# One order table replaced by another: the items of phase one of a pooled attention and Strassen FFN kernel, with more matmuls ahead of the fourth inner step

## The chip, the cores and the metric

The kernel runs on one core of one Trainium2 chip. Its engines are TensorE (PE in the profile, its weight loads PEld), VectorE (DVE), ScalarE (ACT), GpSimd (POOL) and SyncE (SP, which here only issues DMAs). The metric is the device time in microseconds of one execution. The kernel before takes 905.62 us, the median of three runs (904.5 to 905.83).

## The reference

Attention with pooled keys and values, eight batches of eight heads, 576 positions of 64; then a feed-forward layer whose activation is h + sin²(alpha h)/alpha. Cut to what matters, all in float32:

```
q, k, v: (8, 8, 576, 64)
k_p = k.reshape(B, H, 72, 8, D).mean(axis=3)        # 576 keys become 72
v_p = v.reshape(B, H, 72, 8, D).mean(axis=3)
attn = softmax(q @ k_p.T / sqrt(D))                 # 576 x 72 for each head
x = (attn @ v_p) rearranged to (4608, 512)          # 8 batches of 576 tokens, 8 heads of 64
h = x @ w_in                                        # w_in 512 x 2048
g = h + sin(alpha * h)**2 / (alpha + 1e-9)
out = g @ w_out                                     # w_out 2048 x 512
```

## The kernel before, in words

**Two phases.** Phase one computes the attention and, with its output x, the first product h and the activation g, which is stored to memory. Phase two (`outputs`, products at L1294) loads g again and multiplies it by w_out. In the profiled execution phase two begins at 513 us on TensorE. Only phase one is ordered by the table that is changed, apart from a few preparations for phase two (`"R"`: loads and sums that are begun in the last units of phase one).

**Strassen.** The first product is done on blocks of 512 tokens (nine *units* u) and slices of w_in (four values J for each unit). One (u, J) is a *group*, n = 4u + J, 36 in all. A group is a 2 by 2 block product by Winograd's form of Strassen: seven products `M1` to `M7` in place of eight. In each, four parts `M{p}.{i}` (L975) are one matmul instruction each, float32, 128x128 weights and 256 columns; the trace has two records for each. The sums of weights that the products need are made once, the sums of x by `sums_of_x` (L939, VectorE, items `sx` and `sn`). The products share PSUM banks: product 6 is added to a copy of product 1 (`c16`, L950, ScalarE), product 7 to a copy of that (`c67`), and `p5` copies product 5 out. Then come sums on VectorE (`a11`, `a01`, `a00`, `f10`, `f1`; L949), sines (`s..`, L1044) and squares (`q..`, L1051) on ScalarE, and the store of g (`st`, SP).

**The inner level.** In units 1 to 6 products 1 and 5 of some groups are themselves done by seven smaller products (`inner_products`, L1053 on): J=0, 2 and 3 do both, J=1 does product 1 alone. The steps are

- `i.a`: two inner products for each of them into a spare bank (TensorE, L1066)
- `i.ca` and `i.cm`: copies of these on ScalarE, into the result's bank (L1079) and to a buffer (L1083)
- `i.b`: two more, added to what `ca` copied (TensorE, L1066)
- `i.cb`: a copy of one quarter of the result to another (ScalarE, L1086)
- `i.d`: the third inner step on TensorE, added to what `cb` copied (L1066)
- `i.ad`: a sum on VectorE of what is there and what `cm` put aside (L1089)
- `i.e1`, `i.e5`: the fourth inner step on TensorE, added to what `ad` wrote (L1066), one item for product 1 and one for product 5

So each step on TensorE waits for a copy or a sum of what the step before wrote. Other groups' products stand between the steps on TensorE, and under them the copies run.

**The attention** of batch u+1 runs beside the groups of unit u: loads of k, v and q, pooling (`pool_k`, `pool_v`; L271, POOL), scores (L444), softmax (`shift`, `exp`, `norm`), turning of the weights (`turn`, then `move`: 16 DMAs at L650), values (L739, L752), output to x (`out`), and the next but one batch's q turned by VectorE and DMAs (`qa` to `qe`, L357 to L370). The first batch is done by its own finer items (`first_batch`, L1102): q, k and v in pairs of heads, on TensorE `q_head` (L532), `k_head` (L515), `k_last` (L521), `score` (L553), and `fill` (L1131), matmuls on ones whose results nobody reads, between them.

**What sets the order.** Nothing is left to a scheduler. Each item is put on one agenda with a key; `perform` sorts the agenda by the keys and issues the items in that order, and an engine does its instructions in the order of issue. The keys stand in the tables `ORDER` (L42 on). `"F"` is the first batch, `"U0"` the attention items of unit 0, `"U"` those of units 1 to 6, `"U7"` and `"R"` the end. A group's keys are counted from 7n and come from a table by its kind: `first0` to `first3` (unit 0), `enter` (n=4), `mid0` to `mid3` (groups 5 to 26 by their J: 5, 6, 6 and 5 of them), `exit` (n=27), `end0` to `end3` (units 7 and 8).

```
def perform(self, until):
    self.agenda.sort(key=lambda x: x[:2])
    while self.agenda and self.agenda[0][0] < until:
        self.agenda.pop(0)[2]()
```

Of the kernel before, what the change touches and what calls it, by code (L numbers as in the profile page):

```python
# [43 lines left out]
    "load_k0": -3.59252, "load_v": -0.96965, "scores0": 3.279, "shift1": 6.66681, "shift0": 7.14828, "scores1": 7.66855, "shift2": 7.69635,  # L44
    "exp1": 11.39419, "exp0": 11.40344, "shift3": 11.6083, "exp2": 11.66391, "exp3": 11.68798, "norm0": 11.85811, "norm1": 11.86021, "norm2": 11.9294,
    "norm3": 11.93036, "pool_k0": 11.93266, "pool_v": 11.93269, "pool_vm": 11.9327, "turn2": 12.15533, "turn1": 12.33183, "turn3": 12.34767,
    "load_q": 13.4176, "load_k1": 13.54022, "turn0": 15.964, "move": 24.04575, "clean": 24.12855, "qa": 24.12869, "values": 24.12873,
    "out4": 24.12875, "qb": 24.12884, "pool_k1": 24.12885, "out0": 24.12885, "mark": 24.12895, "qc": 24.129, "out2": 24.129, "sx0": 24.1291,
    "inner_x": 24.12915, "out3": 24.33175, "k_t": 24.4364, "k_c": 24.4956, "qd": 24.83712, "out1": 24.87145, "sx1": 24.87995, "qe": 24.96216,
    "sx2": 25.5786, "sx3": 33.62096},  # L50
"F": {
    "load_al": -7.89, "load_q0": -7.88, "sqrt": -7.52, "fill0": -7.4, "turn_al": -7.28, "root": -7.15637, "q_head0": -7.13171, "exp_t": -7.10741,
    "load_k0": -6.95386, "fill1": -6.86584, "load_kr": -6.77452, "refine": -6.57394, "load_k1": -6.56, "load_q2": -6.534, "load_k2": -6.33476,
    "load_k3": -6.22799, "add_k0": -6.06864, "add_r": -5.99534, "load_q4": -5.97084, "load_q6": -5.84, "load_v": -5.76726, "win0": -5.72,
    "k_head0": -5.42865, "k_last": -5.12, "add_k2": -4.77276, "add_k1": -4.54784, "zero_z4": -4.54071, "score0": -4.52, "add_k3": -4.46549,
    "q_head1": -4.4, "zero_tr": -4.37098, "shift0": -4.16, "k_head1": -4.11213, "exp0": -4.04, "fill2": -4.00595, "score1": -3.79101,
    "fill3": -3.70961, "q_head2": -3.56, "qrest": -3.47419, "shift1": -3.44, "exp1": -3.32, "norm0": -3.2, "norm1": -3.08, "fill4": -2.96,
    "k_head2": -2.83714, "k_head3": -2.67519, "q_head3": -2.67509, "vrows": -2.66442, "vrest": -2.65517, "score2": -2.32076, "shift2": -2.24,
    "ahead0": -2.12, "comb0": -2.0, "score3": -1.88, "exp2": -1.85875, "k1_0": -1.79183, "ahead1": -1.76, "shift3": -1.52, "norm2": -1.4,
    "exp3": -1.28, "norm3": -1.16, "values": -1.11464, "load_q1": 0.04, "k1_1": 0.05858, "pool_k0": 1.1349, "win1": 1.89886, "comb1": 1.92786,  # L60
    "comb2": 1.98213, "pool_k1": 3.78556},
"U0": {
    "vsum": 1.50081, "qrest": 1.50141, "ahead": 1.502, "load_v": 2.08618, "pq0": 2.15962, "win3": 2.42169, "vals": 2.503, "sx2": 2.50351,
    "sx3": 2.50375, "score4": 2.504, "pq3": 2.82144, "win2": 2.94801, "pq4": 4.05233, "pq2": 4.0566, "pq1": 4.07221, "qt0": 4.511, "qt1": 4.51172,
    "kt0": 4.51227, "kc0": 4.96887, "scores0": 5.518, "shift0": 5.52, "shift1": 5.521, "comb1": 7.38091, "qt3": 7.92628, "qt2": 8.13953,
    "pool_vm": 8.75569, "qt4": 9.526, "exp1": 9.52613, "exp0": 9.52662, "scores1": 10.519, "shift2": 10.522, "norm0": 12.96627, "shift3": 13.00319,
    "comb2": 13.15659, "norm1": 13.38469, "turn0": 13.38824, "exp2": 14.22682, "exp3": 15.56789, "exp4": 15.57472, "load_k0": 16.01154,
    "load_q": 16.43872, "norm2": 16.65626, "load_k1": 16.66341, "norm3": 16.67159, "comb3a": 16.67343, "turn1": 16.69456, "comb3b": 16.77826,
    "turn3": 17.03674, "turn2": 17.289, "nrest": 17.37323, "move1": 18.86855, "move2": 18.96992, "clean": 18.98312, "move0": 19.548, "arest": 21.5955,
    "qc": 21.89678, "pool_v": 22.64595, "w2_1": 22.78383, "pool_k1": 22.83011, "pool_k0": 22.88021, "qa": 23.561, "qb": 23.562, "qd": 23.84216,  # L70
    "vrest": 26.13943, "values": 26.551, "qe": 26.565, "out0": 26.7312, "out2": 26.9598, "mark": 26.9713, "w2_5": 27.34755, "sn0": 27.5,
    "inner_x": 27.55453, "out1": 27.76959, "out4": 27.8955, "out3": 27.97572, "kt1": 28.19418, "sn2": 28.3493, "sn1": 28.40019, "kc1": 28.50762,
    "sn3": 28.51},
"U7": {
    "sn0": 27.5, "sn2": 27.50625, "sn1": 27.51, "sn3": 28.24964},
"R": {
    "w0": 8.86895, "w1": 11.17262, "w2": 11.21326, "w3": 7.30011, "w4": 17.42295, "w5": 22.96478, "w6": 15.7898, "w7": 16.74706, "w8": 20.6,
    "w9": 22.47405, "w10": 23.6, "v0": 6.6, "v1": 12.9421, "v2": 13.6, "v3": 16.48877, "v4": 17.6, "v5": 20.79675, "g0": 5.5, "i0": 20.16574,
    "i1": 27.65493, "i2": 27.65286, "i3": 27.6628, "o0": 20.58574, "o1": 25.65, "o2": 27.65},
"end0": {  # L80
    "M1.2": -2.57294, "M1.0": -2.53472, "M1.1": -2.45741, "M1.3": -2.25355, "c16": -1.1367, "M5.0": -0.09345, "M5.1": 0.9728, "M2.0": 1.17425,
    "M6.0": 1.17485, "M2.1": 1.21724, "M6.2": 1.21765, "M5.2": 1.21779, "M6.1": 1.21784, "M6.3": 1.21789, "M5.3": 1.21819, "M2.2": 1.21845,
    "c67": 2.29615, "M2.3": 2.3555, "M7.0": 2.35565, "p5": 2.384, "s00": 2.38414, "q00": 2.3842, "M7.1": 2.5708, "M7.2": 2.57295, "M3.2": 3.16644,
    "M3.0": 3.47531, "M3.1": 3.63665, "M7.3": 3.7191, "M3.3": 4.06192, "a00": 6.599, "a11": 6.59915, "M4.0": 6.82409, "a01": 6.89334, "M4.1": 7.01225,
    "M4.2": 7.0125, "s11": 7.04685, "s01": 7.11736, "M4.3": 7.14095, "s10": 7.149, "q1": 7.19287, "q01": 7.22535, "f10": 8.3468, "f1": 8.63666,
    "st": 10.05},
"end1": {
    "M5.0": -3.33019, "M5.1": -2.72125, "M1.0": -0.17668, "M5.2": -0.17606, "M1.1": -0.17602, "M1.2": -0.06105, "M1.3": -0.0, "M5.3": 0.01245,
    "c16": 0.08171, "M6.1": 0.14395, "M6.0": 0.15524, "M6.2": 0.1611, "p5": 0.19815, "M6.3": 0.2009, "M2.1": 0.2077, "c67": 0.20789, "M2.2": 0.20881,
    "M2.3": 0.20922, "M2.0": 0.20955, "s00": 0.3, "q00": 0.3002, "a00": 2.19325, "M7.1": 2.79825, "M3.0": 2.80473, "M7.0": 2.81351, "M7.3": 2.88245,  # L90
    "M7.2": 2.88791, "M3.1": 2.88955, "M3.2": 2.9988, "M3.3": 3.21335, "a11": 3.46515, "s11": 4.32131, "M4.0": 4.4354, "a01": 5.1294, "M4.1": 7.91733,
    "M4.2": 7.92785, "M4.3": 7.99325, "s10": 8.1665, "q1": 8.17037, "s01": 8.2013, "q01": 8.36455, "f10": 9.25247, "f1": 9.6345, "st": 10.05},
"end2": {
    "M5.0": -5.21769, "M5.1": -4.19849, "M1.0": -3.17899, "M1.1": -2.75025, "M1.2": -2.51525, "M1.3": 0.90215, "M5.2": 0.99395, "M5.3": 0.99415,
    "c16": 1.14695, "p5": 1.1828, "M6.0": 1.4299, "M2.0": 1.4318, "M6.2": 1.43214, "M2.1": 1.43255, "M2.2": 1.5857, "M6.1": 1.71475, "M6.3": 1.7193,
    "M2.3": 1.7196, "c67": 1.78765, "s00": 1.78813, "q00": 1.79224, "M7.1": 2.3807, "M3.0": 2.38083, "M7.0": 2.38084, "M7.2": 2.38085, "M7.3": 2.3819,
    "a00": 2.69669, "a11": 2.7835, "M3.1": 3.71335, "M3.2": 3.93591, "M3.3": 5.35825, "M4.0": 5.57345, "a01": 5.76695, "M4.3": 6.28487,
    "M4.1": 6.46705, "M4.2": 7.97136, "s11": 9.31248, "s10": 9.36555, "q1": 9.36695, "s01": 9.43775, "q01": 9.4416, "f1": 9.6118, "f10": 9.90706,
    "st": 10.05},
"end3": {  # L100
    "M5.0": -5.29345, "M5.1": -4.88305, "M1.2": -2.23625, "M1.0": -1.54834, "M1.3": -1.48014, "M5.2": -1.2153, "M1.1": -1.21312, "c16": 2.27975,
    "M6.2": 2.3529, "M6.0": 2.35688, "M6.1": 2.35962, "M2.1": 2.36295, "M2.0": 2.3654, "M6.3": 2.3726, "c67": 2.37425, "M2.2": 2.4012,
# [1468 lines left out]
```

## Time and profile before

| | |
|---|---|
| time, median of three runs | 905.62 us (904.5 to 905.83) |
| span of the profiled execution | 902.2 us |
| time less span (median) | 3.4 us |
| PE busy | 894.0 us, 99% |
| DVE, ACT, POOL busy | 678.2, 457.3, 206.5 us |
| phase two on TensorE | from 513.33 us, 384.23 us |

The page gives the span of one execution and no time of its own for it, so the median stands for it. A row of a timeline has the start, the length, the engine, the line, the operation with its tiles (output <- inputs), its shape and how many instructions it holds, and in brackets how long the engine was idle before and what released it. Matmuls overlap in such rows: a matmul's length is longer than the distance to the next one's start, so the distance between starts is what a matmul costs. In rows of waits the columns are the line that waited, what it waited for, the total in us, the number of times and the longest.

### The profile page before, as it was taken

To read this page: it belongs to the slowest core of one execution; us is meant where nothing else is said; L and a number is where in the kernel's file an instruction comes from. 1 tells how busy PE (TensorE), PEld (TensorE's weight loads), DVE (VectorE), ACT (ScalarE), POOL (GpSimd) and SP (SyncE) were. 2 spreads that over 40 slices of the span, in tenths; PEclk is the share of its full clock that TensorE was granted. 3 is DMA by queue.
4 is the path that set the end of the run, shared out by engine and by line. 5 is a ranking of instruction groups with operands and counts; after the bars stand their busy time and mean duration, and the time that the engine had idled before them with its cause. 6 is when DMAs were issued, how large, how long until landed. Compare 5 with 4: busy or idle time off the path is not lost.

```text
span 902.2 us, 18350 instructions
## 1 busy us (share of the span) xinstructions
PE 894.0 (99%) x7146; PEld 815.0 (90%) x7146; DVE 678.2 (75%) x1016; ACT 457.3 (51%) x1073; POOL 206.5 (23%) x235
## 2 busy tenths in 40 slices
PE   8999999999999999999999999999999999999997
PEld 5787888978888898888888899999999999999997
DVE  7576857668586684854466999979798888889894
ACT  5696878868787787786885611211111111111111
POOL 4969561814418164130000000000000000000000
PEclk9999999999999999999999999999999999999999
DMA  9956766666766666645426346261618172534401
GB/s 271 229 170 181 209 193 177 209 173 200 212 179 197 198 187 173 175 133 200 181 104 213 99 152 193 65 191 35 224 30 231 31 201 63 171 92 130 134 15 40
DMA packets 128751, 141.17 MB, mean 156 GB/s; under 512 B 46920, under 2 KB 95704, under 8 KB 128664
## 3 DMA queue, kind: packets, MB, share of 16 engines
q1 hardware_dynamic: 125880, 137.88, 52.6%
q10 hardware_dynamic: 2784, 2.11, 0.9%
q8 instruction: 57, 0.93, 0.4%
q14 instruction: 30, 0.25, 0.1%
HBM read 75.37 MB, written 47.19 MB: 136 GB/s over the span
## 4 chain that ended last, share of the span: by engine, by line
PE 98%; DVE 1%; DMA 0%; ACT 0%; issue 0%; ACTq 0%
PE PS L1294 43%; PE PS L975 41%; PE PS L1066 7%; PE PS L444 2%; PE PS L739 2%; PE PS L752 1%; DVE home L939 1%; DMA q<-in_q_dram 0%; PE PS L553 0%; PE PS L532 0%; PE PS L1131 0%; PE PS L416 0%; PE PS L697 0%; PE PS L343 0%; PE PS L695 0%; PE PS L607 0%
## 5 line engine op out<-in xcount | busy, mean ns | idle before, releaser
L975 PE MATMUL PS<-home,a 128*128 128x256 f32 x968 | 250.3, 382 | 0.0
L975 PEld LDWEIGHTS PS<-home,a 128*128 128x128 f32 x968 | 177.3, 190 | 28.6 <-issue 4.7
L975 PE MATMUL PS<-home,as 128*128 128x256 f32 x728 | 194.9, 381 | 0.9 <-DVE home L939 0.9
L975 PEld LDWEIGHTS PS<-home,as 128*128 128x128 f32 x728 | 134.1, 190 | 18.3 <-DVE home L939 0.9
L1294 PE MATMUL PS<-s,wb 128*128 128x144 f32 x896 | 119.1, 286 | 0.0
L1294 PEld LDWEIGHTS PS<-s,wb 128*128 128x128 f32 x896 | 113.6, 190 | 0.0
L1051 ACT ACTIVATE s<-s,c 128x256 f32<-128x256 f32 (+1 forms) x216 | 112.7, 580 | 0.0
L1344 POOL TENSOR_TENSOR cc<-cc,cb 128x576 f32<-128x576 f32 x1 | 2.0, 1974 | 483.1 <-DVE cb L1249 483.1
L949 DVE TENSOR_TENSOR h<-PS,s 128x512 f32<-128x512 f32 x72 | 49.5, 687 | 70.3 <-ACT s L1051 70.3
L1430 ACT COPY PS<-PS 128x144 f32<-128x144 f32 x56 | 14.7, 263 | 143.4 <-PE PS L1294 140.8
L1294 PE MATMUL PS<-r,wb 128*128 128x144 f32 x512 | 73.2, 286 | 0.0
L1294 PE MATMUL PS<-s,a 128*128 128x144 f32 x512 | 73.2, 286 | 0.0
L1044 ACT ACTIVATE s<-h,al 128x256 f32<-128x256 f32 x144 | 64.1, 502 | 16.4 <-DVE h L949 13.3
L271 POOL TENSOR_TENSOR kvin<-kvin 96x768 f32<-96x768 f32 (+3 forms) x42 | 69.9, 1665 | 3.1 <-DMA a<-in_moe_w_in_dram 0.6
L1294 PEld LDWEIGHTS PS<-r,wb 128*128 128x128 f32 x512 | 67.1, 190 | 0.1
L1294 PEld LDWEIGHTS PS<-s,a 128*128 128x128 f32 x512 | 67.1, 190 | 0.0
L949 DVE TENSOR_TENSOR h<-PS,p 128x512 f32<-128x512 f32 x72 | 49.1, 685 | 22.3 <-PE PS L975 21.7
L950 ACT COPY PS<-PS 128x512 f32<-128x512 f32 x72 | 41.4, 576 | 46.2 <-PE PS L975 23.0
L1044 ACT ACTIVATE s<-PS,al 128x256 f32<-128x256 f32 x144 | 60.3, 473 | 6.1 <-PE PS L975 5.8
L498 POOL TENSOR_TENSOR ex<-ex,sm 128x576 f32<-128x576 f32 (+1 forms) x28 | 35.2, 1270 | 109.8 <-DVE sm L497 108.9
L1412 ACT COPY PS<-PS 128x144 f32<-128x144 f32 x56 | 14.7, 263 | 88.7 <-PE PS L1294 88.7
L949 DVE TENSOR_TENSOR h<-h,s 128x1024 f32<-128x1024 f32 x36 | 44.8, 1246 | 14.2 <-ACT s L1051 14.1
(217 smaller groups left out, 1531.4 us busy)
## 6 DMA issues: line engine op xcount, KB each, us to landing
g_bridge<-h SPq DMA_DIRECT2D x72, 512.0 KB
r<-g_bridge SPq DMA_DIRECT2D x31, 1152.0 KB
out_dram<-o SPq DMA_DIRECT2D x122, 72.0 KB
kvin<-in_k_dram SPq DMA_DIRECT2D x14, 576.0 KB
q<-in_q_dram SPq DMA_DIRECT2D x7, 1024.0 KB
kvin<-in_v_dram SPq DMA_DIRECT2D x14, 512.0 KB
ex<-tr SPq DMA_DIRECT2D x54, 92.0 KB
ex<-tr SPq DMA_DIRECT2D x54, 88.0 KB
```

What stands on the lines that cost most here:

```text
L271: self.nc.gpsimd.tensor_tensor(out=t[..., 0:w] if w > D else out, in0=t[..., 0:w], in1=t[..., w:2 * w], op=OP.add)
L444: nc.tensor.matmul(ps[e][r0 + r:r0 + r + q.shape[-1], h, :], q[s], kb[s, hp, :], start=True, stop=True)
L498: nc.gpsimd.tensor_tensor(out=E(i), in0=E(i), in1=sm.unsqueeze(2).to_broadcast([P, n, Sp]), op=OP.mult)
L739: nc.tensor.matmul(o[r:r + 64], w, x, start=start and i < 2, stop=False, skip_group_check=True)
L949: add = lambda o, x, y: nc.vector.tensor_tensor(out=o, in0=x, in1=y, op=OP.add)
L950: copy = lambda o, x: nc.scalar.copy(out=o, in_=x)
L975: nc.tensor.matmul(ps[:, jj, :], self.A[p][:, kk, f * P:(f + 1) * P], x[:, kk, :], start=start and p not in G.begun, stop=(kk == 1), skip_ ...
L1044: self.nc.scalar.activation(out=G.s()[:, i, jj, j, :], in_=src[:, jj], func=AF.Sin, scale=self.al[:, f:f + 1])
L1051: self.nc.scalar.activation(out=x, in_=x, func=AF.Square, scale=self.c[:, f:f + 1])
L1066: nc.tensor.matmul(out, W[m][:, G.J], self.X2[p][m], start=start, stop=True, skip_group_check=True)
L1294: nc.tensor.matmul(out, W[:, J // 2, J % 2, :], A[:, J, :], start=(start and J == 0), stop=(J == self.NJ - 1), skip_group_check=True)
L1412: nc.scalar.copy(out=st["x1"][:, 1, :], in_=st["x1"][:, 0, :])
```

## The change

All keys of all tables are replaced. The items are the same 2072, with the same tiles, and nothing else in the program differs but for the length of the tables (later lines move by 13). The order within an engine changes in many places. On TensorE around inner steps (unit 2, the items between b and e; `9.M7.2` is part 2 of product 7 of group 9):

```
before
 10.i.b  9.M7.2 9.M7.3  10.i.d  9.M3.2 9.M3.3 9.M4.0  10.i.e1
 11.i.b  10.M4.0 10.M3.3  11.i.d  10.M4.1 10.M4.2  11.i.e1 10.M4.3 11.i.e5
 12.i.b  11.M3.3 11.M4.0  12.i.d  11.M4.1 11.M4.2  12.i.e5 12.i.e1
after
 10.i.b  9.M3.1  10.i.d  9.M3.0 9.M3.3 9.M4.0  10.i.e1 10.i.e5
 11.i.b  10.M3.2  11.i.d  10.M4.0 10.M3.3 10.M4.2  11.i.e1 10.M4.1 10.M4.3 11.i.e5
 12.i.b  11.M4.0  12.i.d  11.M3.3 11.M4.1 11.M4.2  12.i.e5 12.i.e1
```

Counted over all groups with an inner level: between `b` and `d` the parts of products number two at all 23 places before; after, one at 17 places (J=0, J=2, J=3 and `exit`) and two at the six of J=1. Between `d` and the first `e` there are two at 12 places (J=0, J=3, `exit` and group 5) and three at 11 (the other J=1, J=2) before; after, three at 18 places and four at five (J=1 but group 5). Between `a` and `b` there are three before and two after in J=0, six and four in J=3.

In the first batch `load_q0` goes behind `sqrt` (an activation with a table load) on the ACT queue, `fill1` goes ahead of `q_head0`, and `exp_t`, an activation that loads the Exp table early, goes behind the real exps. In unit 0 `move1` (DMAs issued on the ACT queue) goes behind the last group's `c67`. In the units `pool_k0` goes ahead of the norms, `sx0` ahead of `qb`, and the last group's store stands among the q DMAs on SP.

The diff, cut to the tables of which the above speaks (of the groups' tables their first rows, which hold the inner steps):

```diff
 ORDER = {
 "U": {
...
-    "norm3": 11.93036, "pool_k0": 11.93266, "pool_v": 11.93269, "pool_vm": 11.9327, "turn2": 12.15533, "turn1": 12.33183, "turn3": 12.34767,
-    "load_q": 13.4176, "load_k1": 13.54022, "turn0": 15.964, "move": 24.04575, "clean": 24.12855, "qa": 24.12869, "values": 24.12873,
-    "out4": 24.12875, "qb": 24.12884, "pool_k1": 24.12885, "out0": 24.12885, "mark": 24.12895, "qc": 24.129, "out2": 24.129, "sx0": 24.1291,
...
+    "exp1": 11.4537863, "shift3": 11.5606739, "exp2": 11.5749813, "load_v": 11.6634649, "pool_k0": 11.6641341, "exp3": 11.6756746, "exp0": 11.6792958,
+    "norm0": 11.6815954, "norm1": 11.829592, "norm2": 11.8296945, "norm3": 11.8297241, "turn1": 11.9371184, "pool_v": 12.2512783, "turn3": 12.2512868,
+    "turn2": 12.2512961, "load_q": 12.2513439, "load_k1": 13.1706876, "clean": 14.054537, "turn0": 14.5781539, "pool_vm": 15.3881202,
+    "pool_k1": 16.5643388, "move": 18.6575401, "qc": 22.342905, "qa": 23.8784224, "values": 23.9152365, "out4": 24.3459226, "out0": 24.3621729,
+    "out2": 24.4751143, "out3": 24.4910334, "sx0": 24.7828496, "k_t": 24.7858031, "qb": 24.9987446, "k_c": 25.0126124, "inner_x": 25.0147734,
...
 "F": {
-    "load_al": -7.89, "load_q0": -7.88, "sqrt": -7.52, "fill0": -7.4, "turn_al": -7.28, "root": -7.15637, "q_head0": -7.13171, "exp_t": -7.10741,
-    "load_k0": -6.95386, "fill1": -6.86584, "load_kr": -6.77452, "refine": -6.57394, "load_k1": -6.56, "load_q2": -6.534, "load_k2": -6.33476,
...
+    "load_k0": -1000000000.9774988, "load_al": -1000000000.7203386, "sqrt": -680942032.6472147, "load_q0": -593140306.5683773,
+    "load_kr": -295016958.0402516, "fill0": -118296725.9662964, "fill1": -112740380.1011902, "load_k1": -111236418.7229699,
+    "load_q2": -111056995.502221, "turn_al": -77566422.4392492, "add_k0": -22062511.3033825, "add_r": -12942322.436592, "zero_tr": -12199830.8370804,
+    "q_head0": -11880703.2116935, "root": -2049949.9456236, "load_k2": -1460156.5858616, "k_head0": -432006.9175994, "load_k3": -270302.5751315,
...
+    "exp3": -1.9731635, "norm2": -1.9731385, "norm3": -1.6171014, "values": -0.1459929, "k1_1": 0.2131822, "qrest": 0.382981, "load_q1": 0.389824,
+    "exp_t": 0.6753617, "comb1": 0.6941198, "zero_z4": 0.7093044, "comb2": 1.9354651, "pool_k0": 2.0283551, "win1": 2.5722239, "pool_k1": 2.5903328},
...
 "exit": {
-    "i.a": -5.02158, "i.ca": -4.768, "i.cm": -4.76115, "i.b": -4.15145, "i.cb": -3.5502, "i.d": -3.09985, "i.ad": -3.09835, "i.e1": -2.6215,
+    "i.a": -6.2908975, "i.ca": -5.9063401, "i.cm": -5.6284411, "i.b": -5.3735849, "i.cb": -4.3517993, "i.d": -3.2662028, "i.ad": -1.9978099,
...
 "mid0": {
-    "i.a": -3.44775, "i.ca": -3.11535, "i.cm": -3.1115, "i.b": -3.11065, "i.cb": -3.1106, "i.d": -2.748, "i.ad": -1.9601, "i.e5": -0.69805,
+    "i.a": -2.7162159, "i.ca": -2.7161198, "i.b": -2.7092763, "i.cm": -2.6445356, "i.cb": -2.5335258, "i.d": -2.5050542, "i.ad": -2.2004668,
+    "i.e5": -1.5756361, "i.e1": -1.5527523, "p5": -0.3504135, "c16": -0.0804385, "M6.0": 5.7545124, "M2.2": 5.922828, "M2.3": 6.0770388,
...
 "mid1": {
-    "i.a": 4.34025, "i.ca": 4.3997, "i.cm": 4.40437, "i.b": 4.4051, "i.cb": 4.40681, "M5.0": 4.41522, "i.d": 4.41525, "i.ad": 4.61795,
-    "M5.2": 4.68665, "M5.1": 4.68679, "i.e1": 4.68728, "c16": 4.6958, "M2.0": 4.71385, "M6.1": 4.7738, "M6.2": 4.77608, "M6.3": 4.77889,
...
+    "i.a": 4.4832034, "i.ca": 4.4995236, "i.cm": 4.5463919, "i.b": 4.5573799, "M5.0": 4.557869, "i.cb": 4.5729051, "i.d": 4.6195236,
+    "i.ad": 4.6615495, "M5.2": 4.6629099, "M5.1": 4.6633747, "i.e1": 4.6797383, "M5.3": 4.6800828, "c16": 4.6854214, "M6.0": 4.829568,
...
 "mid2": {
-    "i.a": -2.3038, "i.cm": -1.76102, "i.ca": -1.7514, "i.b": -1.7503, "i.cb": -1.7501, "i.d": -1.735, "i.ad": -1.59855, "i.e1": -1.0348,
+    "i.a": -2.3201018, "i.cm": -1.8950209, "i.ca": -1.7487989, "i.b": -1.7486477, "i.cb": -1.6947681, "i.d": -1.4040893, "i.ad": -1.3557013,
+    "i.e1": -0.2380127, "i.e5": -0.2347519, "c16": -0.227342, "p5": -0.1727754, "M6.3": 0.5708463, "M6.1": 0.5770216, "M6.0": 0.5776212,
...
 "mid3": {
-    "i.a": -5.44769, "i.cm": -5.07042, "i.ca": -4.6089, "i.b": -4.1596, "i.cb": -3.09295, "i.d": -3.08935, "i.ad": -3.08745, "i.e1": -2.73575,
+    "i.a": -6.3045532, "i.ca": -6.1240003, "i.b": -5.178015, "i.cb": -5.1162205, "i.d": -3.8780599, "i.cm": -2.4359572, "i.ad": -1.4270429,
+    "i.e1": -1.229432, "c16": 1.6817633, "i.e5": 2.7143651, "M2.1": 2.7152937, "M6.2": 2.7157457, "p5": 2.7160902, "M6.3": 2.7625862,
...
```

## The prediction

> **What bounds the kernel now.** I read the engine shares and the slices first, then the chain of waits, the idle times, and the timeline around one inner step. The shares and the slices of the page:
>
> ```profile
> PE 894.0 (99%) x7146; PEld 815.0 (90%) x7146; DVE 678.2 (75%) x1016; ACT 457.3 (51%) x1073; POOL 206.5 (23%) x235
> PE   8999999999999999999999999999999999999997
> PE 98%; DVE 1%; DMA 0%; ACT 0%; issue 0%; ACTq 0%
> ```
>
> TensorE is busy 99% of the span, and the chain that ended last is TensorE for 98% of it. The work on TensorE is the same before and after, so only its gaps can change the time: those at the start (first slice, an 8), and gaps inside "busy" that a share doesn't show. In the chain, phase two is one stretch of matmuls:
>
> ```profile
> 513.33 384.23 PE PS L1294 x3136
> ```
>
> No key in the changed tables reaches into that loop; those 384 us stay. What can change lies before 513 us. What the weight loads (PEld) and TensorE wait for:
>
> ```profile
> PEld PS L1066 <- DVE PS L1089: 4.2, 11, 0.4
> PEld PS L975 <- ACT PS L950: 1.4, 7, 0.2
> PE PS L532 <- DMA q<-in_q_dram: 1.0, 1, 1.0
> PE PS L975 <- DVE home L939: 0.9, 2, 0.5
> ```
>
> The first row is the fourth inner step (L1066) waiting for the addition at L1089, 11 times. The timeline of one inner step, unit 2, group 11 (start, length, engine, line):
>
> ```profile
> 180.50 0.39 PE L1066 MATMUL PS<-home,a 128*128 128x128 f32 x2
> 180.72 0.60 PE L975 MATMUL PS<-home,a 128*128 128x256 f32 x2
> 180.98 0.36 ACT L1086 COPY PS<-PS 128x256 f32<-128x256 f32 x1 [1.01 <-PE PS L1066]
> 181.16 0.59 PE L975 MATMUL PS<-home,as 128*128 128x256 f32 x2
> 181.39 0.40 PEld L1066 LDWEIGHTS PS<-last,q 128*128 128x128 f32 x2
> 181.59 0.38 PE L1066 MATMUL PS<-last,q 128*128 128x128 f32 x2
> ...
> 182.03 1.03 PE L975 MATMUL PS<-home,a 128*128 128x256 f32 x4
> 182.29 0.70 DVE L1089 TENSOR_TENSOR PS<-PS,m 128x512 f32<-128x512 f32 x1 [0.80 <-issue]
> 183.04 0.30 PEld L1066 LDWEIGHTS PS<-home,aM 128*128 128x128 f32 x2 [0.38 <-DVE PS L1089]
> 183.05 0.49 PE L1066 MATMUL PS<-home,aM 128*128 128x128 f32 x2
> 183.37 0.39 PE L1066 MATMUL PS<-ex,a 128*128 128x128 f32 x2
> ```
>
> Starts tell what is lost, not ends (ends are modelled). A product (two L975 records) takes 0.43 to 0.44 us of issue: 180.72, 181.16, then d at 181.59. Between b and d stand two products, and under them the copy cb (L1086) is hidden: b's last record ends 180.89, cb runs 180.98 to 181.34, d's weights load at 181.39, d is due 181.59. Its slack is 0.20 us. Between d and e stand two products too, and that is not enough: due 182.90, e starts 183.05.
>
> **The sum, part by part**, against the profiled execution: span 902.2 us. The three times (904.5 to 905.83, median 905.62) leave 2.3 to 3.6 us around a span; I take the median's 3.4 as unchanged.
>
> *Three products ahead of e.* In groups J=0, J=3 and the exit group (5+5+1 = 11) e gets a third product. Lost now at each: 0.15 late (183.05 against 182.90), and 0.10 because the weights of the next pair aren't loaded ahead (183.05 to 183.37 is 0.32, usual 0.22). 11 x 0.255 = 2.8 us. With three, e is due at 183.33, 0.29 after the addition ends; J=2 has three before and shows no such wait. Worth -2.8 (at least the bare lateness, -1.65).
>
> *One product less ahead of d.* The tables pay for that third product out of the place before d: in J=0, J=2, J=3 and exit (17 places) one product stands between b and d, two before; the six of J=1 keep two. Then d is due at 181.16, while cb can't end earlier: it waits for b's last record, and b does not move. d's weights load at 181.39: 0.23 late, plus 0.10 for weights that aren't hidden, as at e. 0.34 x 17 = +5.8. Ends: 17 x 0.23 = 3.9 if the weights stay hidden, 5.9 at 0.35, the largest such reading; e's row is the nearest, of the same line and operand shape, so I take 0.34. Nothing else hides it: queued behind d on TensorE stand all later products, in order.
>
> *First step and its copy.* In J=0 one product less stands between a, ca and b: some 0.07 x 5 = +0.35 (0 to 0.7).
>
> *Copies c16 and c67 (L950).* Twelve places leave two products between the releaser and its user, and 13 such copies cost 6 x 0.095 and 7 x 0.066 us (read as above from starts). After, the least distance is nearly three. -1.0 (-1.0 to 0).
>
> *The units' attention on other queues.* The normalisation and turn chain feeds a11's consumer through VectorE, idle 1.2 us ahead of it; pool_k0 goes ahead of the norms into 18 us of idle POOL; the 16 DMAs of move (SP, from 173.31 to 183.9) land by 185.43, values start 187.25. All that is covered: 0. On SP, 14 of the 16 q DMAs (L370) start some 3.7 us later since sx0 stands before qb on VectorE. They land 202.22 now, scores1 starts 205.3; with 0.6 us more of the store between them, about 1 us of cover is left. 0, but that cover is thin (rival three).
>
> *The start.* load_q0 goes behind the sqrt table load and its activation on the ACT queue: issue 1.24 becomes 2.75, and with its 3.4 us to landing q0 is there at 6.15, not 4.63. But fill1 (4 matmuls, now at 5.58 to 7.49) moves ahead of it:
>
> ```profile
> 1.24 0.48 ACTq L224 DMA_DIRECT2D q<-in_q_dram  x1
> 1.75 1.28 ACT L1135 ACT_TABLE_LOAD   x1 [1.75 <-issue]
> 4.67 1.11 PE L532 MATMUL PS<-ident,q 128*128 128x128 f32 x4 [1.01 <-DMA q<-in_q_dram]
> 5.58 1.91 PE L1131 MATMUL PS<-full 128*128 128x512 bf16 x4
> 8.90 0.73 PE L553 MATMUL PS<-h,q 64*64 64x72 f32 x32 [0.30 <-DVE home L314]
> ```
>
> The fills then take 1.06 to 4.9, q_head0 6.15 to 7.05, k_head0 and k_last to 8.3, the first scores 8.65 against 8.90: about -0.2 (-1.7 if the landing is shorter and k's addition early, +1.5 if q0's delay comes through whole). The Exp table load, no longer made early, adds 1.28 ahead of the first exp; its sum is used 1.43 later: 0 (0 to 0.9). The Trainium skill, "ScalarE: Activation LUTs", "What happens when an `exp` ACTIVATE runs", puts a table load with its drain at about 2.7 us, by which q0 would land some 1.4 later still and the sum be 909.7; here the row is 1.28, and the activation behind it starts at 3.04, right at its end.
>
> *First unit.* Product counts ahead of M5.0 and M6.0, which wait for sums of x (1.4 us with their reloads), are the same. move1 goes behind c67 on the ACT queue and lands 3.7 us after issue; a11 and M4.0 of the last group wait behind it with 8.8 us against about 9 us. +0.3 (-1 to +3).
>
> *End of phase one.* Two preparations for phase two stand ahead of a11 on VectorE: +0.2 (0 to 0.5).
>
> Sum: 5.8 + 0.35 - 2.8 - 1.0 = +2.35 in the steady part; -0.2 + 0.3 + 0.2 outside. +2.65: a span of 904.9, a time of **908.3 us**.
>
> **Rivals.**
> 1. *d is not late (other side).* If cb's copy can start or end 0.23 us earlier, so that it is done inside one product (it needs 0.50 from b's end to d's weights, of which 0.09 and 0.05 are hand-over), d's term falls to nothing and the rest stands: 0.35 - 2.8 - 1.0 + 0.3 = -3.15, 902.5 us. For: the ends are modelled, and cb itself is only 0.36. Against: cb's start follows b's end at the same 0.09 at each place I read. The sign turns at 0.185 us lost per place, and below 0.08 the gain exceeds 1.8 us. Chance 0.17.
> 2. *Only the bare wait.* 0.23 x 17 = 3.9, and the rest as above: 3.9 + 0.35 - 3.8 + 0.3 = +0.75, 906.4 us, no change. For: a single product in front may let the sequencer load d's weights early. Against: e's rows show 0.32 in the same situation. 0.15.
> 3. *An attention wait comes through.* scores1 waits for the late q DMAs in five units (0.6 to 0.9 each, 3 to 4.5), or M4.0 in the first unit: 908.3 + 3.7 = 912.0 us. For: 1 us of cover at SP's later start. Against: SP has idle time there. 0.15.
> 4. *A quicker clock at the start.* The spacing of TensorE is 0.427 us (fills) up to 8.39 us and half of that after; a 1.0 us gap at 3.66 breaks the early work. With nine fills in one stretch of 3.84 us the full speed might be granted before q_head0, and q_head0, k_head0 and k_last (2.15 us) would take half: -1.1, 907.2 us, within no change. The Trainium skill, "TensorE: Matmul & The Clock Gate", "Part 1: The HAM clock gate", says that the slow clock is released after about 3.4 us of sustained activity and that the window runs free; the gap and the switch at 8.39, 3.7 us after 4.67, agree with it. 0.08.
>
> **How the numbers follow.** The forecast has the remaining 0.45; its own range is 907.4 to 910. 0.2% of the time (1.8 us) is about what a measurement of this kernel can tell from no change: 903.8 to 907.4 counts as same. Faster: rival 1, 0.17. Same: rivals 2 and 4, 0.23. Slower: the forecast and rival 3, 0.60. The range leaves out the outer halves of rivals 1 and 3 (0.16 in all): 902.5 to 912.0.
>
> **What would show it.** In the changed profile: d's weight loads (L1079, was L1066) waiting for ACT L1099 (was L1086) some 17 times and the DVE wait gone; from the start of b's last pair to that of d about 0.89 us in place of 1.09 (180.50 to 181.59), where 0.65 would mean no wait; the L975 wait for ACT L950 gone; first scores near 8.65; phase two 384 us. The prediction is wrong if d shows no lateness (rival 1), or if waits for L370's DMAs stand before scores or L975.

## The result, and the profile after

The changed kernel takes 928.32 us (median of four runs, 927.11 to 930.41) against 905.06 us for the kernel before in the same comparison: a ratio of 1.0262, 95% interval 1.0244 to 1.0279. It is 23 us slower; the forecast was 2.7 us slower, and the time lies 16 us above its range.

The first lines of the page of the changed kernel (a slice is 23 us here; in all fences `...` and jumps in the start times stand for rows left out):

```profile
span 928.7 us, 18348 instructions
PE 905.5 (98%) x7146; PEld 820.8 (88%) x7146; DVE 676.9 (73%) x1016; ACT 455.9 (49%) x1071; POOL 211.1 (23%) x235
PE   5999999999999999999999999999999999999997
PEclk6999999999999999999999999999999999999999
```

The profiled execution is the longest of the four (930.41 us), and the kernel before's is a short one of its kind (902.2, where the spans of its executions run from 902.0 to 905.1); so the spans differ by 26.5 us and the medians by 23. The first slice tells most: TensorE is half idle in it. Its granted clock reads 0.6, where the page before reads 0.9 or more; but that row also reads full where nothing was recorded, as in the first 8.4 us before, where the fills are as slow as here (0.427 us apart). The lengths of the matmuls are the safer sign. The idle times, of TensorE and (last line) of its weight loads:

```profile
PE PS L545 <- DMA q<-in_q_dram: 8.8, 1, 8.8
PE PS L457 <- DMA q<-tr: 3.8, 4, 1.6
...
PE PS L1079 <- ACT PS L1099: 0.8, 5, 0.2
...
PEld PS L1079 <- ACT PS L1099: 5.6, 12, 0.5
```

One wait of 8.8 us for q, where it was 1.0; scores (L457, was L444) waiting for q's turned rows, a row that wasn't there; and the third inner step waiting for cb (L1099). The row of the fourth step's wait (4.2 us, 11 times) has shrunk to 0.3 us, once. The inner step of group 11 again:

```profile
195.18 0.39 PE L1079 MATMUL PS<-home,a 128*128 128x128 f32 x2
195.40 0.60 PE L988 MATMUL PS<-home,as 128*128 128x256 f32 x2
195.65 0.36 ACT L1099 COPY PS<-PS 128x256 f32<-128x256 f32 x1 [0.47 <-PE PS L1079]
196.06 0.30 PEld L1079 LDWEIGHTS PS<-last,q 128*128 128x128 f32 x2 [0.47 <-ACT PS L1099]
196.06 0.49 PE L1079 MATMUL PS<-last,q 128*128 128x128 f32 x2
196.39 0.39 PE L1079 MATMUL PS<-ex,aM 128*128 128x128 f32 x2
...
197.91 0.38 PE L1079 MATMUL PS<-home,aM 128*128 128x128 f32 x2
```

From b's last pair to d it is 0.88 us, as forecast (0.89); d's second pair follows 0.33 later in place of 0.22; and e, at 197.91, waits for nothing.

I followed the start times of the same TensorE instructions through both traces, and sorted the excess over each instruction's usual spacing by place. The sum is that of these two executions, some 3 us more than between the medians. In us, changed less before:

| part | forecast | measured |
|---|---|---|
| start, to the last scores of the first batch (17.8, now 29.1) | -0.2 | +11.3 |
| rest of the first unit, to 97 us | +0.3 | -1.0 |
| d waits for cb, 17 places | +5.8 | +6.0 |
| e waits for the addition | -2.8 | -2.6 |
| b waits for ca | +0.35 | +2.7 |
| between products (copies c16, c67) | -1.0 | +0.1 |
| scores and what they wait for | 0 | +5.3 |
| values | 0 | +2.6 |
| smaller places up to 513 us | 0 | -0.35 |
| end of phase one and the first 60 us of phase two | +0.2 | +2.1 |
| sum, last matmul | +2.65 | +26.2 |

### The profile page after: what moved, and what is told of

Read it like the earlier page. It is cut to its first block, busy times and chain, and to the rows that moved or that the text cites. A ratio compares the mean times of both kernels' runs of the same rounds, so it can differ in the third digit from the quotient of the medians.

```text
span 928.7 us, 18348 instructions
## 1 busy us (share of the span) xinstructions
PE 905.5 (98%) x7146; PEld 820.8 (88%) x7146; DVE 676.9 (73%) x1016; ACT 455.9 (49%) x1071; POOL 211.1 (23%) x235
## 4 chain that ended last, share of the span: by engine, by line
PE 88%; DMA 4%; SPq 3%; DVE 3%; ACT 1%; issue 1%; ACTq 0%; DVEq 0%
PE PS L1307 39%; PE PS L988 35%; PE PS L1079 6%; SPq L383 3%; PE PS L752 2%; DMA q<-tr 1%; PE PS L457 1%; DMA r<-g_bridge 1%; PE PS L765 1%; DMA q<-in_q_dram 1%; DVE h L962 1%; DVE x L1262 1%; ACT PS L1099 1%; SPq L1112 0%; DMA home<-in_k_dram 0%
## 5 line engine op out<-in xcount | busy, mean ns | idle before, releaser
L988 PE MATMUL PS<-home,a 128*128 128x256 f32 x968 | 247.0, 380 | 0.0
L988 PEld LDWEIGHTS PS<-home,a 128*128 128x128 f32 x968 | 179.3, 190 | 27.1 <-issue 4.7
L962 DVE TENSOR_TENSOR h<-PS,s 128x512 f32<-128x512 f32 x72 | 48.8, 684 | 76.0 <-ACT s L1064 67.9
L284 POOL TENSOR_TENSOR kvin<-kvin 96x768 f32<-96x768 f32 (+3 forms) x42 | 72.1, 1717 | 59.4 <-DMA kvin<-in_k_dram 57.2
L1057 ACT ACTIVATE s<-PS,al 128x256 f32<-128x256 f32 x144 | 60.2, 470 | 14.6 <-PE PS L988 14.1
L962 DVE TENSOR_TENSOR h<-h,s 128x1024 f32<-128x1024 f32 x36 | 48.8, 1356 | 14.4 <-ACT s L1064 14.2
L962 DVE TENSOR_TENSOR h<-PS,p 128x512 f32<-128x512 f32 x72 | 48.4, 680 | 10.9 <-PE PS L988 8.6
L1307 PE MATMUL PS<-x,wb 128*128 128x144 f32 x384 | 55.0, 286 | 0.3 <-DVE x L1262 0.3
```

The lines of the kernel that those rows point to most:

```text
L284: self.nc.gpsimd.tensor_tensor(out=t[..., 0:w] if w > D else out, in0=t[..., 0:w], in1=t[..., w:2 * w], op=OP.add)
L962: add = lambda o, x, y: nc.vector.tensor_tensor(out=o, in0=x, in1=y, op=OP.add)
L988: nc.tensor.matmul(ps[:, jj, :], self.A[p][:, kk, f * P:(f + 1) * P], x[:, kk, :], start=start and p not in G.begun, stop=(kk == 1), skip_ ...
L1057: self.nc.scalar.activation(out=G.s()[:, i, jj, j, :], in_=src[:, jj], func=AF.Sin, scale=self.al[:, f:f + 1])
L1307: nc.tensor.matmul(out, W[:, J // 2, J % 2, :], A[:, J, :], start=(start and J == 0), stop=(J == self.NJ - 1), skip_group_check=True)
```

## The experiments

### The start: q0's load alone, both ways

The chain of waits of the changed kernel over its first 20 us (start, length, what):

```profile
2.10 4.27 DMA home<-in_k_dram
6.39 7.29 DMA q<-in_q_dram
13.73 1.12 PE PS L545 x4
```

load_q0 was issued not at 2.75 us, when the ACT queue was through with the table load and its activation, but at 6.39, when a transfer of k landed. In the trace every DMA of the start names one of eight semaphores (counters) that it raises when it lands. The first eight DMAs of both queues together carry no wait; each later one waits until the DMA eight places ahead, which has the same semaphore, has landed. q0 is now the twelfth and waits for the fourth, the k transfer of 2.10; in the kernel before it was the third, at 1.24, and waited for nothing. By its key it is still the third load; what put it twelfth in that list isn't shown. I tested it both ways. In the changed kernel:

```diff
 "F": {
-    "load_q0": -593140306.5683773,
+    "load_q0": -700000000.0,
```

> The changed kernel with one key altered: load_q0 stands ahead of the sqrt item again, so q0's load is the second DMA on the ACT queue and waits for no earlier transfer. Theory (q0's load waited for the fourth transfer to land, was issued at 6.39 us and landed at 13.7, and everything else followed): q_head0 starts near 5 us instead of 13.73, the first scores near 8.7 instead of 16.3, and some 10.5 us come back: 917.8 us. Rival (the other moves in the first batch, such as the fills, zero_z4, exp_t, the later loads, cost as much by themselves): the first stretch stays over 5 us late and the time over 923 us.

Measured: 916.66 us (914.86 to 918.07), ratio 1.0120 (1.0103 to 1.0138); 11.7 us came back. The timeline:

```profile
1.06 4.02 PE L1144 MATMUL PS<-full 128*128 128x512 bf16 x9 [1.06 <-DVE full L1476]
1.23 0.48 ACTq L237 DMA_DIRECT2D q<-in_q_dram  x1
...
5.22 1.11 PE L545 MATMUL PS<-ident,q 128*128 128x128 f32 x4
7.62 0.73 PE L566 MATMUL PS<-h,q 64*64 64x72 f32 x32 [0.30 <-ACT h L535]
```

q_head0 now waits for nothing, and the first scores come 1.28 us before those of the kernel before. The other way, in the kernel before:

```diff
 "F": {
-    "load_q0": -7.88,
+    "load_q0": -7.45,
```

> The kernel before with one key altered: load_q0 goes behind the sqrt item, as in the changed kernel, and nothing else moves. Theory (the wait for an earlier transfer, not the table load, makes it late): issue near 6.4 us, landing after 10 us, TensorE idle for 6 to 9 us, 913 to 917 us. Rival (only the 1.5 us of table load and activation, as the prediction had it): issue near 2.75 us, landing near 6.2, 905.5 to 907 us.

Measured: 913.54 us (912.95 to 915.26), ratio 1.0087 (1.0072 to 1.0102). Its chain:

```profile
2.11 4.20 DMA home<-in_k_dram
6.33 7.11 DMA q<-in_q_dram
13.48 1.12 PE PS L532 x4
```

The same wait, and a landing 0.2 us earlier; the rival's 2.75 us is refuted. The first scores are 8.8 us late and the last matmul 9.1 (7.8 between the medians). Issued at 6.33, q0 takes 7.1 us to land, against 3.4 when issued at 1.24. By then k, v and w_in are on their way: from 5 to 10 us of this run the DMA engines move 307 GB/s at a share of 1.06, before that 134 at 0.50. That the crowd makes it slow fits this, but wasn't tried by itself.

### The fills alone

The kernel before with fill1 where the changed kernel has it:

```diff
 "F": {
-    "fill1": -6.86584,
+    "fill1": -7.35,
```

> The kernel before with the four fill matmuls fill1 ahead of turn_al and q_head0, as in the changed kernel, and load_q0 where it was. Theory (q0 lands at 4.63 us while the nine fills run, and the work behind it moves up by the fills' time): first scores about 1.0 us earlier, 904.6 us. If the clock rises sooner with the fills in one stretch, q_head0's four matmuls take 0.55 us in place of 1.1 and another 0.5 to 1.1 us go. Rival (the DMAs of k and q that come next set the end of the start): the gain is gone by 20 us, 905.6 us.

Measured: 906.47 us against 905.75, ratio 1.0013 (1.0004 to 1.0022): slightly slower, not 1 us faster. Its timeline and its windows (length, busy time of each engine with its instructions, granted clock, DMA share, GB/s):

```profile
5.23 0.66 PE L532 MATMUL PS<-ident,q 128*128 128x128 f32 x4
...
7.94 0.66 PE L515 MATMUL PS<-twos,home 128*128 128x64 f32 x4 [2.05 <-DVE home L316]
10.01 1.24 PE L553 MATMUL PS<-h,q 64*64 64x72 f32 x32 [0.30 <-ACT h L522]
```

```profile
5.00:10.00 5.00, 2.24 (x12) 1.62 (x11) 4.11 (x14) 2.38 (x5) 1.83 (x4) 0.86 1.08 324
10.00:15.00 5.00, 5.00 (x75) 4.00 (x76) 2.50 (x4) 1.43 (x3) 2.26 (x3) 0.50 1.11 317
```

The fills did raise the clock sooner in this execution: q_head0 takes 0.66, not 1.11 (in q0_first, with the same nine fills, it still took 1.11). But then TensorE waits 2.05 us for k's addition, with no fill left to lay there, the granted clock falls to 0.50, and the first scores take 1.24 in place of 0.73. The addition itself is late: on VectorE it stands behind the sums on alpha, and these wait for turn_al, which the fills put off from 3.40 to 5.01. The Trainium skill, "TensorE: Matmul & The Clock Gate", "Part 1: The HAM clock gate", says that activity releases the clock, and that an idle window of some 3.4 us takes it back. Here the clock fell at 8.6 us (from the 0.86 of the first row), and the 3.4 us before that were mostly, not wholly, idle: they hold 1.3 us of matmuls. The rule had a chance of its own in the prediction, and I had it work in one direction only. The fall is not the whole of it: of the ten executions five have a mean clock of 0.995 to 0.996, as the profiled one (907.47), and take 906.37 to 908.02; the five at 0.998 to 1.000 take 905.83 to 906.51, and aren't 1 us faster than before either.

In the changed kernel the 8.8 us gap does the same on a larger scale:

```profile
20.00:25.00 5.00, 5.00 (x52) 3.95 (x50) 3.78 (x7) 3.17 (x5) 1.31 (x2) 0.52 0.51 101
25.00:30.00 5.00, 5.00 (x109) 3.94 (x112) 2.79 (x6) 2.87 (x7) 1.67 (x2) 1.00 0.53 159
```

The slow matmuls last from 13.73 to some 24.7 us. In q0_behind, where fill1 still stands behind q_head0, they end sooner after the same gap: its first scores, at 17.70, take 0.73. That the four fills there make this difference is likely from these rows, not shown by a run of its own.

### d alone, e alone, and both

The kernel before with d one product earlier at the 17 places:

```diff
-"mid0" "i.d": -2.748     "mid2" "i.d": -1.735      "exit" "i.d": -3.09985
+"mid0" "i.d": -2.979425  "mid2" "i.d": -1.737435   "exit" "i.d": -3.24427
-"mid3" "i.cb": -3.09295, "i.d": -3.08935
+"mid3" "i.cb": -3.25,    "i.d": -3.23481
```

> The kernel before with one thing altered: at the 17 places where the changed kernel does so, the third inner step stands one product earlier, so that one product lies between b and d in place of two, and the one passed now lies ahead of the fourth step. Theory of the prediction (0.34 us lost at each d, 0.255 gained at 11 e): +5.8 - 2.8 = +3.0, 908.7 us. Rival (only the bare 0.23 us at each): +1.1, 906.8 us. Rival (d isn't late): -2.8, 902.9 us.

Measured: 917.32 us (915.61 to 918.21), ratio 1.0130 (1.0116 to 1.0144), +11.7 and not +3.0. In the trace d's wait is 6.2 us and e's at J=0, J=3 and exit is gone, as the theory has it. The rest is at J=2, and in the products:

```profile
PEld PS L975 <- ACT PS L950: 7.6, 12, 1.6
...
PEld PS L1066 <- ACT PS L1086: 5.7, 12, 0.6
...
PEld PS L975 <- DVE h L949: 3.1, 7, 0.8
```

The copies of L950 are late because a sum on VectorE is. The same sum and GpSimd's pooling beside it, in this kernel, and then in the kernel before:

```profile
175.62 2.36 POOL L271 TENSOR_TENSOR kvin<-kvin 128x1024 f32<-128x1024 f32 x1
176.30 2.76 DVE L949 TENSOR_TENSOR h<-h,s 128x1024 f32<-128x1024 f32 x1
```

```profile
170.66 1.22 DVE L949 TENSOR_TENSOR h<-h,s 128x1024 f32<-128x1024 f32 x1
170.74 3.36 POOL L271 TENSOR_TENSOR kvin<-kvin 128x1024 f32<-128x1024 f32 x1
```

Whichever begins first is short, and the other waits for it: before, VectorE was 0.08 us ahead. The later d, and the addition behind it on VectorE, turned that round, five times (2.76 to 3.25 us), and sines, c67 and the next products waited. The Trainium skill, "SBUF — State Buffer", "SBUF: two separate sides", has the rule: the two engines share a pair of ports, and the first holds it for its whole instruction. To see that this is the excess, the same without J=2:

```diff
-"mid2" "i.d": -1.737435
+"mid2" "i.d": -1.735
```

> The kernel before with d one product earlier at J=0, J=3 and exit only (11 places); J=2 keeps two products ahead of d. In the kernel with all 17, some 7 us came from J=2's groups, where VectorE's sum of 1024 columns began while GpSimd's pooling ran and took 2.76 us in place of 1.22, so that sines and the copy c67 behind it were late. Theory (that collision, not the 17 waits themselves, makes the excess over 3 us): 11 x 0.35 - 2.8 = +1.0, 906.7 us, and no long wait of L975 for L950. Rival (each earlier d delays the work behind it in every group): over 910 us.

Measured: 906.77 us against 904.83, ratio 1.0015 (1.0006 to 1.0025), as the theory has it; in the trace +1.15 us from 97 to 403 us. L975's wait for L950 is back at 1.4 us, as before, and from 97 us on no sum takes 2 us. So d's and e's prices hold where nothing stands behind them.

The third product ahead of e, alone, in the kernel before (p5 and c16 go along in J=0, since they copy what e makes):

```diff
-"mid0" "i.e5": -0.69805, "p5": 2.55425, "i.e1": 2.87235, "c16": 2.92563
+"mid0" "i.e5": 3.075,    "p5": 3.095,   "i.e1": 3.085,   "c16": 3.1
-"mid3" "i.e1": -2.73575   "exit" "i.e1": -2.6215,   "i.e5": -2.5921
+"mid3" "i.e1": -0.1594    "exit" "i.e1": -2.3328375 "i.e5": -2.105925
```

> The kernel before with one thing altered, the one that the change is named for: at the 11 places of J=0, J=3 and exit the fourth inner step stands one product later, so that three products lie ahead of it, and the two between b and d stay. Theory (a third product hides the addition, and nothing else there is short): the 11 waits for the addition at 0.255 us go, -2.8 us, 902.9 us. Rival (each product moved there is missing elsewhere, and a copy c16 or a wait further on takes its place): 905 us or more.

Measured: 908.75 us (907.96 to 910.25), ratio 1.0041 (1.0028 to 1.0053): slower by 3.2. The inner steps lost 2.7 us of waits, as expected. But the product that went ahead of e had been the cover of the copies behind e:

```profile
202.22 0.56 ACT L950 COPY p<-PS 128x512 f32<-128x512 f32 x1
202.83 1.33 PE L444 MATMUL PS<-kblk,q 64*64 64x72 f32 x64 [0.72 <-ACT p L950]
```

```profile
185.38 0.57 ACT L950 COPY PS<-PS 128x512 f32<-128x512 f32 x1 [1.58 <-PE PS L1066]
186.00 1.13 PE L975 MATMUL PS<-home,a 128*128 128x256 f32 x4 [0.26 <-ACT PS L950]
```

In J=0 scores wait 0.88 us for p5, five times (4.4); in J=3 and exit a product waits 0.42 for c16, six times (2.5). The rival holds for this place.

The same gain from a place that can spare it: at J=3 and exit there are six products between a and b. b and d go one product earlier, e stays:

```diff
-"mid3" "i.b": -4.1596, "i.cb": -3.09295, "i.d": -3.08935   "exit" "i.b": -4.15145, "i.d": -3.09985
+"mid3" "i.b": -4.169,  "i.cb": -3.245,   "i.d": -3.235     "exit" "i.b": -4.169,   "i.d": -3.24427
```

> The kernel before with b and d of J=3 and exit each one product earlier and e where it was: two products between b and d, three between d and e, and the product comes from the six between a and b instead of from behind e. Theory (a third product ahead of e is worth 0.255 us where the place it is taken from can spare it): six waits go, -1.5 us, 904.1 us, and the copies c16 keep their cover. Rival (any such move opens a wait elsewhere, as moving e did): no gain or slower.

Measured: 904.61 us (902.57 to 905.51) against 905.75, ratio 0.9989 (0.9980 to 0.9999): faster, by 1.1 us, with an interval that just excludes no change. In the trace the stretch from 97 to 403 us is 1.55 shorter, and e (184.44) waits for nothing after the addition:

```profile
183.40 0.70 DVE L1089 TENSOR_TENSOR PS<-PS,m 128x512 f32<-128x512 f32 x1 [0.36 <-issue]
184.44 0.38 PE L1066 MATMUL PS<-home,aM 128*128 128x128 f32 x2
```

This version beats both kernels, the one before narrowly. Last, the changed kernel with d and e each one product later (two between b and d, at least three between d and e):

```diff
-"mid0" "i.d": -2.5050542, "i.e5": -1.5756361, "i.e1": -1.5527523   "mid3" "i.d": -3.8780599, "i.e1": -1.229432
+"mid0" "i.d": -2.288815,  "i.e5": -0.9004252, "i.e1": -0.6270963   "mid3" "i.d": -2.4440002, "i.e1": -0.2209918
-"mid2" "i.d": -1.4040893, "i.ad": -1.3557013, "i.e1": -0.2380127, "i.e5": -0.2347519   "exit" "i.d": -3.2662028, "i.e1": -1.9070044
+"mid2" "i.d": -1.0257869, "i.ad": -1.0,       "i.e1": -0.2295559, "i.e5": -0.2288179   "exit" "i.d": -2.4440003, "i.e1": -0.2209918
```

> The changed kernel with the third and the fourth inner step of J=0, J=2, J=3 and exit each one product later: two products between b and d again, three between d and e. Theory (d's wait for the copy costs 0.35 us at 17 places, and nothing waits behind it): -6.0, 922.3 us. Rival (other waits of the new order stand behind these and take the time up): over 925 us.

Measured: 925.21 us (924.23 to 926.06), ratio 1.0219 (1.0206 to 1.0233), 3.1 below the changed kernel's median. In the trace the inner steps' waits fall from 10.2 to 4.5 us, nearly the 6.0 of the theory; but in J=0 scores now wait 0.44 for p5, five times (2.2), since e stands right ahead of them. So the theory holds for the waits themselves, and the rival, with its "over 925 us", for the time.

### scores waiting for q's turned rows

On SP the store of J=2's group (L1112) stands among the q DMAs (L383), and scores1 starts when the last has landed (changed kernel, unit 1):

```profile
154.34 1.97 SPq L1112 DMA_DIRECT2D g_bridge<-h  x2
156.36 5.97 SPq L383 DMA_DIRECT2D q<-tr  x8
```

```profile
165.38 0.99 PE L457 MATMUL PS<-kblk,q 64*64 64x72 f32 x46 [1.55 <-DMA q<-tr]
```

Taking the store from there:

```diff
 "mid2": {
-    "st": 11.8667562,
+    "st": 12.3,
```

> The changed kernel with one key altered: the store of the group J=2 goes behind the last eight q DMAs (qe) on SP instead of ahead of them. Theory (scores1 waits because these eight stand behind the store's 2 us of issue): the waits of scores for q (1.71, 0.41, 0.16, 0.58, 1.72 us in units 1 to 5) shrink by up to 2 us each, all of them gone: 923.7 us. Rival (the DMAs are late because sx0 stands ahead of qb on VectorE, and the store only fills the time that SP waits anyway): the waits stay within 0.5 us of these, 927 to 929 us.

Measured: 927.41 us (925.01 to 928.85), ratio 1.0234 (1.0217 to 1.0252), not told apart from 1.0262 (1.0244 to 1.0279). The waits of scores for q are all gone from the trace, 4.6 us, but by 403 us only 2.2 of them are won. New ones stand there:

```profile
PE PS L988 <- ACT PS L963: 1.1, 2, 1.0
...
PE PS L1079 <- ACT PS L1092: 0.9, 2, 0.5
```

What causes the wait is shown; that removing it is worth its length is not.

### The end: the preparations for phase two

Phase two of the changed kernel has four waits in its first 50 us. From its chain: the load of r21, and the last of the sums behind it.

```profile
541.81 8.35 DMA r<-g_bridge
...
560.33 2.48 DVE r L1262
```

Two kernels, the changed one with the table R of before, and with R, U7 and end0 to end3 of before:

```diff
-"R": {"w0": 7.5948058, ...}      (of the changed kernel)
+"R": {"w0": 8.86895, ...}        (of the kernel before)
```

> The changed kernel with the table R (the preparations for phase two) taken from the kernel before. Theory (phase two's first four stalls, 0.37, 0.68, 0.56 and 0.61 us, come from where R's VectorE sums and loads now stand among the last groups' work): they go, 926.2 us. Rival (they come from the new order of the last groups' own items, so that the last store and the load of r21 are late): the stalls stay, 928 us.

Measured: 937.26 us (936.22 to 937.87), ratio 1.0344 (1.0329 to 1.0360), 9 us slower than the changed kernel. A product waits 5.5 us for a copy of L962 in the last groups: in the chain of waits R's sums run on VectorE ahead of the sum (L961) that the work before this copy waits for. So R's sums and these groups share VectorE, and each order fits its own partner only. Neither theory had that.

```diff
-"R", "U7", "end0", "end1", "end2", "end3" of the changed kernel
+"R", "U7", "end0", "end1", "end2", "end3" of the kernel before
```

> The changed kernel with the tables R, U7 and end0 to end3 all taken from the kernel before, since R alone made a wait of 5.5 us for a copy in the last groups. Theory (phase two's 2.2 us of stalls come from how the last groups and the preparations stand to each other): they go, and the copies c16 of the last groups wait 7 x 0.066 us again: 926.5 us. Rival (they come from phase one being later as a whole against its DMAs): they stay, 928.5 us.

Measured: 927.27 us (925.62 to 928.26), ratio 1.0241 (1.0226 to 1.0255). By its time the run isn't told apart from the changed kernel (1.0244 to 1.0279). In the trace the four waits are gone, 2.1 us between 537 and 600 us. So they belong to the pair of R and the last groups, and not to a late phase one.

### All four together

The changed kernel with the edits of the runs above (load_q0, the store, the end's tables, d and e):

```diff
+"F" "load_q0", "mid2" "st", the tables of the end, "i.d" and "i.e" as in the four diffs above
```

> The changed kernel with all four alterations at once: load_q0 ahead of sqrt, the store of J=2 behind qe, the tables of the end from before, d and e one product later. Theory (these four causes hold nearly all of the loss): 928.3 less 11.7 for the start, 2.1 for phase two, 5.8 for d and 0 to 4 for the q DMAs: 905 to 909 us. Rival (other waits of the new order make up for what is removed): over 911 us.

Measured: 913.17 us (909.97 to 914.27), ratio 1.0079 (1.0059 to 1.0099). 15 of the 23 us are accounted for; the theory wanted at least 19, and the rival (over 911) holds. In the profiled execution (909.97, the fastest of the four and 3.2 us below their median; where those 3.2 lie no trace shows) the start is even with before by 97 us (-0.1) and nothing is lost after 403; what is left, +6.4, lies in between: values +3.3, scores behind e's p5 copy 2.2, and smaller ones. So some 6 us of the new order of the units, and 7 by the medians, aren't in the four causes. What makes values late (their rows wait for sines, copies and the DMAs of move) was not tried by itself.

## Why the prediction was wrong, point by point

- **The start (-0.2, with a bound of +1.5) is the step that failed**: +11.3. "Issue 1.24 becomes 2.75" looked at the ACT queue alone; it was 6.39, behind the landing of a k transfer. I read what stands ahead of load_q0 on its queue, but not what its DMA would wait for once other transfers are ahead of it in the program. Then "with its 3.4 us to landing" took the duration from an empty moment; it was 7.1 to 7.3 five microseconds later. At the first scores the loss is 7.4 us, by issue and landing; the other 3.9 come up to the last scores of the first batch, up to 24.7 us at the slow clock. Up to 2.0 of the 11.3 may be the kernel before's early clock in its profiled execution (last section).
- **The third product ahead of e: right** (-2.8, measured -2.6), as were the places.
- **One product less ahead of d: right**, 0.34 at each, 5.8 in sum, measured 6.0. Rivals one and two, d not late or only the bare 0.23, are refuted: the reload of the weights comes to 0.08 to 0.11 at every place.
- **The first step and its copy: mis-sized**, 0.35 against 2.7. J=0 had 0.19 in place of 0.07. J=3 went from six products between a and b to four, and I costed that at nothing: ca, which stands behind other work on ScalarE, ended at 194.35 with b due at 194.30: 0.23 at each of five places, with the weights. One more place, at 111 us, lost 0.5.
- **Copies c16 and c67: the waits named went, and as many came**: +0.1 for -1.0.
- **The units' attention, "all that is covered: 0": wrong.** scores1 did wait, as rival three has it, for the DMAs that I had left 1 us of cover, with up to 1.7 us at one place; I took it for a rival at 0.15. For values I read 1.8 us of slack between a landing and its use, and 2.6 us were lost there; the cause of those stays open.
- **End of phase one: the wrong place.** The groups themselves lost nothing, but phase two's first waits cost 2.1: "no key in the changed tables reaches into that loop" holds for its instructions and not for the loads and sums that it starts from.
- **The base**: around the span lie 1.7 us in the four runs of the changed kernel (930.41 against 928.7), not 3.4.
- **Rival four (the clock)** was incomplete: with nine fills in one stretch q_head0 ran fast in one execution (0.66) and slow in another (1.11), and a gap behind them let the clock fall again.

## What to carry to other kernels

In an order this tight a product is cover for several waits at once: before moving one, look at what it covers where it now stands, on both sides, and take it from a place with more than it needs (six products, not two). Price a moved DMA by its completion waits and by its landing at its new time, not by the instructions ahead of it on its queue. And a sum of local waits holds only while no other engine's order turns over: an earlier d with its price of 0.35 us cost 1.3 us in total (by the ratio) with e's gain at eleven places, and 10 more at six others, where at five it let GpSimd start first.

## What the runs showed of the hardware that I had not expected

- A VectorE sum of 128x1024 takes 1.22 us, and 2.76 to 3.25 when a GpSimd operation of 2.36 us on the same memory has begun a moment before it; the other way round GpSimd's takes 3.36.
- In the same first 20 us of the kernel before, unchanged there, TensorE reaches full spacing at 8.4 us in two traces (before, e_later) and at 12.8 to 14.1 in three others (d_earlier_not_j2, mid3_three, d_earlier; only later tables are altered in these runs): first scores of 0.73 or 1.24 us, and the third scores 1.5 to 2.0 us later (15.57 against 17.06 to 17.59). That is as much as the whole gain of a mended inner step. The granted clock reads 1.00 in the first 30 us of all five.
